# Attention scores on halves of the TensorE array, with PSUM banks split 4/2/2

## The chip, the cores and the metric

The kernel runs on one core of a Trainium2 chip. The core has five engines that work side by side and meet through semaphores: TensorE (PE, matrix products into PSUM), VectorE (DVE), ScalarE (ACT), GpSimd (POOL) and SyncE (SP, which issues DMAs). PSUM has eight banks of 2 KB per partition; every matmul result lands in one of them and must be read out by DVE or ACT before the bank can be used again. The metric is the device time of one execution in microseconds; three runs of the kernel before gave 281.81, 282.52 and 284.34 us, median 282.52.

## The reference

Two layers follow each other. The first is attention with 4 batches, 8 heads, 768 positions and head size 64, in which a query sees the 8 first keys (global) and the 96 latest ones (local), with a bias by distance:

```python
scores = scale * np.matmul(q, k.transpose(0, 1, 3, 2))
keep = is_global | is_local          # key < 8, or 0 <= query - key < 96
bias = -slopes[:, None, None] * dist[None, :, :]
scores = np.where(keep, scores + bias, -1e9)
a = softmax(scores)                  # over the keys
x = np.matmul(a, v)                  # then heads side by side: 768 x 512 per batch
```

The second mixes positions by a matrix of rank 32 and then channels by a feed-forward of width 2048:

```python
h = x.transpose(0, 2, 1) @ U @ V
u = x + h.transpose(0, 2, 1)
out = u + np.maximum(u @ w_ch1, 0.0) @ w_ch2
```

## The kernel before, in words

The work unit of the attention is a pair of heads of one batch, 16 pairs in all, four per batch. Keys run along partitions. A pair's q and k arrive as 128 positions by (head, 64) tiles; `st_T` transposes six blocks of q and six of k on PE (line 223) into two PSUM tiles `tp`, so that head 0 lies on partitions 0 to 63 and head 1 on 64 to 127. DVE copies the k tile whole into `kT` (L230) and builds `kA` from it (L231, L232), which holds for each off-diagonal block the local keys with the eight global ones put in front. The q tile is copied into two zero-padded tiles: ACT copies head 0 into the upper half of `qz..0` (L229), DVE copies head 1 into the lower half of `qz..1` (L235); the other halves were set to zero once. So a score matmul for one head can contract over all 128 partitions of `kT`, both heads' keys, and the zeros drop the other head.

A head has 11 score blocks of 128x128: six diagonal (L263, from `kT`) and five beside the diagonal (L268, from `kA`), written into `sc` tiles of up to four blocks, so three chunks per head. For pairs 4 to 15 (batches 1 to 3) `st_S` evicts each chunk on DVE with scale and bias into `sp` (L294), `st_E` takes the exp of a head on ACT (L302, into `ep`), and `st_V` multiplies `ep` with the values (L314, L318, into `ob`), divides by the sum and writes x (L323, L325, L328). For pairs 0 to 3 (batch 0) `st_SE` adds the bias with a matmul over all 128 rows and takes the exp straight from PSUM.

`st_M1` and `st_M2` do the low-rank mix (`tmp_ps` L336, `ups` L347 and L352; the results `uT` go out on DVE for one half of the positions, L358, and on ACT for the other, L360). The feed-forward of a batch is a queue of units: 32 up units of four `hps` matmuls (L376) and a relu on ACT (L380, into `htr`), and 24 down units of `cps` matmuls (L389, L395), four units to a token tile, which ends with an addition on DVE (L401) and a store.

PSUM tiles come from three pools: `sc` (scores) with three banks, `oc` (`ob`, `cps`) with two, `th` (`tp`, `tmp_ps`, `ups`, `hps`) with three. A pool's banks go round in the order of allocation; an operation that needs a bank waits until its last reader is done.

Batch 0 is issued in the order in which it is written. After `ordered.close()` a scheduler orders the instructions of each engine ahead of time; the program loops over pairs 4 to 15, and `fill` puts feed-forward units of the batch before between the steps of the attention. What runs on the chip is then a fixed order per engine; PE executes its matmuls in that order. After the last pair the feed-forward of batch 3 runs alone: per half batch 16 up units in a row, then 12 down units.

Of the kernel before, what the change touches and what calls it, by code (L numbers as in the profile page):

```python
# [11 lines left out]
FP32 = mybir.dt.float32  # L12
FP16 = mybir.dt.float16
# [3 lines left out]
ALU = mybir.AluOpType  # L17
# [3 lines left out]
def kernel(  # L21
# [13 lines left out]
    nc = tc.nc  # L35
    B, H, S, D = q.shape
    NG = int(n_global)
    NL = int(n_local)
    P = 128
    DM = H * D  # L40
    NSB = S // P
# [4 lines left out]
    NP = H // 2  # L46
    qk_scale = 1.0 / math.sqrt(D)
# [5 lines left out]
    slope = [2.0 ** (-8.0 * (h + 1) / H) for h in range(H)]  # L53
# [5 lines left out]
    W = 256 * NSB - P  # L59
# [6 lines left out]
    kp = ctx.enter_context(tc.tile_pool(name="kp", bufs=2))  # L66
    scp = ctx.enter_context(tc.tile_pool(name="scp", bufs=2))
# [3 lines left out]
    psum = ctx.enter_context(tc.tile_pool(name="psum", bufs=1, space=bass.MemoryType.PSUM))  # L71

    def ps_sc():
        return psum.tile([P, 512], FP32, name="sc", tag="sc", bufs=3)

    def ps_oc(name):
        return psum.tile([P, 512], FP32, name=name, tag="oc", bufs=2)

    def ps_th(name, dtype=FP32, cols=512):
        return psum.tile([P, cols], dtype, name=name, tag="th", bufs=3)  # L80


    NVB = 4
# [30 lines left out]

    NPAIR = B * NP
    staged, cast, vts = {}, {}, {}


    ordered = ExitStack()
# [9 lines left out]
    def warm(n):  # L129
# [12 lines left out]
        out=relB, in_=relB, compare_op=ALU.is_ge, fill=BIG,  # L142
# [3 lines left out]
        out=relB, in_=relB, compare_op=ALU.is_ge, fill=BIG,  # L146
# [24 lines left out]
    relcat = cst.tile([P, 3, 256], FP32, name="relcat")  # L171
# [39 lines left out]
    kts, kas, vas = {}, {}, {}  # L211

    def st_T(i):
        stq, stk = cast.pop(i)
        kT = kp.tile([P, S], FP16, name="kT", tag="kT")
        kA = kp.tile([P, NSB - 1, P], FP16, name="kA", tag="kA")
        tps = []
        for st in (stq, stk):

            tp = ps_th("tp", FP16, S)  # L220
            tps.append(tp.rearrange("d (n p) -> d p n", n=NSB))
            for n in range(NSB):
                nc.tensor.matmul(  # L223
                    tp[:, n * P:(n + 1) * P], st[:, n].rearrange("s h d -> s (h d)"), ident16,
                    is_transpose=True, start=(n == 0), stop=(n == NSB - 1),
                )
        tq, tk = tps
        z = qz[i % 2]
        nc.scalar.copy(z[0][0:D].rearrange("d (p n) -> d p n", n=NSB), tq[0:D])  # L229
        nc.vector.tensor_copy(kT.rearrange("d (p n) -> d p n", n=NSB), tk)  # L230
        nc.vector.tensor_copy(kA.rearrange("d n p -> d (n p)"), kT[:, 0:S - P])  # L231
        nc.vector.tensor_copy(  # L232
            kA[:, 1:, 0:NG], kT[:, 0:NG].unsqueeze(1).broadcast_to((P, NSB - 2, NG))
        )
        nc.vector.tensor_copy(z[1][D:P].rearrange("d (p n) -> d p n", n=NSB), tq[D:P])  # L235
        kts[i], kas[i] = kT, kA
# [11 lines left out]
    sps, eps = {}, {}  # L248

    def scores(i, hi, c, on_pe):  # L250
        h = 2 * (i % NP) + hi
        kT, kA, z = kts[i], kas[i], qz[i % 2][hi]
        sc = ps_sc()
        c0 = 512 * c
        tot = min(512, W - c0)
        r0 = 256 if c else 0
        if on_pe:
            nc.tensor.matmul(
                sc[:, 0:tot], slI[:, h], rel16.rearrange("p a c -> p (a c)")[:, r0:r0 + tot], start=True, stop=False
            )  # L260
        for kb in (2 * c, 2 * c + 1):
            o = 256 * kb - c0
            nc.tensor.matmul(  # L263
                sc[:, o:o + P], kT[:, kb * P:(kb + 1) * P], z[:, kb * P:(kb + 1) * P],
                start=(o == 0 and not on_pe), stop=(o + P == tot),
            )
            if kb < NSB - 1:
                nc.tensor.matmul(  # L268
                    sc[:, o + P:o + 2 * P], kA[:, kb], z[:, (kb + 1) * P:(kb + 2) * P],
                    start=False, stop=(o + 2 * P == tot),  # L270
                )
        return sc, c0, tot, r0
# [10 lines left out]
            )  # L283

    def st_S(i, c):
        if c == 0:
            sps[i] = [
                scp.tile([P, W], FP32, name=f"sp{hi}", tag=f"sp{hi}", bufs=1)
                for hi in range(2)
            ]  # L290
        relf = relcat.rearrange("p a c -> p (a c)")
        for hi in range(2):
            sc, c0, tot, r0 = scores(i, hi, c, False)
            nc.vector.scalar_tensor_tensor(  # L294
                out=sps[i][hi][:, c0:c0 + tot], in0=sc[:, 0:tot],
                scalar=qk_scale / slope[2 * (i % NP) + hi], in1=relf[:, r0:r0 + tot],
                op0=ALU.mult, op1=ALU.add,
            )
# [32 lines left out]
    def st_M1(i):  # L331
        b, dc = i // NP, i % NP
        ch = slice(dc * P, (dc + 1) * P)
        tps = ps_th("tmp_ps")
        for n in range(NSB):
            nc.tensor.matmul(  # L336
                tps[:, 0:P], u16[:, n], x16s[b][:, n, ch],
                start=(n == 0), stop=(n == NSB - 1),
            )
        nc.vector.tensor_copy(tmps[b][:, ch], tps[:, 0:P])  # L340

    def st_M2(i):
        b, dc = i // NP, i % NP
        ch = slice(dc * P, (dc + 1) * P)
        for g in range(2):
            ups = ps_th("ups")
            nc.tensor.matmul(  # L347
                ups[:, 0:GT], tmps[b][:, ch], v16w[:, g * GT:(g + 1) * GT],
                start=True, stop=False,
            )  # L350
            for t in range(NTG):
                nc.tensor.matmul(  # L352
                    ups[:, t * P:(t + 1) * P], x16s[b][:, NTG * g + t, ch], ident16,
                    start=False, stop=(t == NTG - 1),
                )
            dst = uTs[b][:, dc, g * GT:(g + 1) * GT]
            if g == 0:
                nc.vector.tensor_copy(dst, ups[:, 0:GT])  # L358
            else:
                nc.scalar.copy(dst, ups[:, 0:GT])  # L360
# [56 lines left out]
    new_batch(0)  # L417
    cast_qk(0, nc.vector)
    st_T(0)
    warm(2)  # L420
    cast_qk(1, nc.vector)
# [6 lines left out]
    for i in range(NP):  # L428
# [12 lines left out]
        if i:  # L441
            cast_qk(i + 2, nc.gpsimd)
        st_SE(i, 1)
        st_T(i + 1)
        if i < 3:
            slopes(2 * i + 2, 2 * i + 4)
# [27 lines left out]
    for i in range(NP, NPAIR):  # L474
# [6 lines left out]
        for c in range(3):  # L481
            st_S(i, c)
            fill(1)
# [8 lines left out]
        if i + 1 < NPAIR:  # L492
            if hp == NP - 1:
                new_batch(b + 1)
            st_T(i + 1)
# [48 lines left out]
```

## Time and profile before

| what | value |
|---|---|
| three runs, us | 281.81, 282.52, 284.34 |
| span of the profiled execution, us | 279.8 |
| PE busy, us | 255.3 (91%) |
| DVE busy, us | 147.8 (53%) |
| ACT busy, us | 123.2 (44%) |
| POOL busy, us | 87.2 (31%) |
| mean granted PE clock | 0.963 |

The span runs from the first to the last instruction of the profiled execution; its own device time is not listed, the median of the three runs is 2.7 us above the span. The page gives, for each group of instructions, the line, the engine, the operation, what it writes and reads, the count, then busy time in us, the mean duration in ns, and the idle time of the engine just before with what ended it. Matmuls are pipelined: the 228 ns of a score matmul is from its start to its modelled end, while the next one may start 56 ns later. In the timeline each row has its start and duration in us. About 57 us pass until batch 0 is through; from there to 232.8 us attention and feed-forward share PE, and the last 47 us are feed-forward alone.

### The profile page before, as it was taken

The page shows a single profiled execution, that of the slowest core. Times are in us where ns is not written, and L with a number is a line of the kernel's source. Part 1 is how long each engine was busy: PE and PEld are TensorE (multiplying, and loading weights), DVE is VectorE, ACT ScalarE, POOL GpSimd, SP SyncE. Part 2 cuts the span into 40 slices and gives each one's busy share as a digit, 9 for nine tenths or more (in the row PEclk, how much of TensorE's full clock was granted, in tenths as well). Part 3 has the DMA queues.
Part 4 walks back from the last instruction along what each step waited for, and adds up shares of the span by engine and source line. Part 5 has one row for each costly group of instructions (what it writes and reads, how often), then busy time and mean ns, then how long its engine had stood idle before and what let it go on. Part 6 is the DMA issues. An engine that isn't in the chain of part 4 may idle for free.

```text
span 279.8 us, 5080 instructions
## 1 busy us (share of the span) xinstructions
PE 255.3 (91%) x2076; PEld 156.1 (56%) x2076; DVE 147.8 (53%) x301; ACT 123.2 (44%) x209; POOL 87.2 (31%) x129
## 2 busy tenths in 40 slices
PE   7765775899998999799999999999999999999994
PEld 3544554566556655566456655675566555545541
DVE  6766799156666564755957575754574440010011
ACT  2434551565218650668037630856076604604700
POOL 8948688360425124330606042300200010000000
PEclk9779896699999999999999999999999999999999
DMA  6999999992462527170634023000110021001001
GB/s 220 277 281 181 198 233 235 227 239 25 150 105 15 128 63 152 55 127 2 164 79 40 2 43 64 37 2 0 75 41 0 2 76 40 0 37 75 2 37 75
DMA packets 42327, 26.64 MB, mean 95 GB/s; under 512 B 26912, under 2 KB 39232, under 8 KB 42304
## 3 DMA queue, kind: packets, MB, share of 16 engines
q0 software_dynamic: 30144, 7.44, 27.5%
q1 hardware_dynamic: 12160, 18.88, 20.0%
q8 instruction: 16, 0.26, 0.4%
q14 instruction: 7, 0.06, 0.1%
HBM read 27.46 MB, written 6.29 MB: 121 GB/s over the span
## 4 chain that ended last, share of the span: by engine, by line
PE 62%; DVE 8%; ACT 4%; issue 2%; ACTq 0%
PE hps L376 25%; PE cps L395 24%; ACT ep L302 3%; PE tp L223 3%; DVE sp L294 2%; PE sc L268 2%; PE cps L389 2%; PE sc L263 2%; DVE qz L235 2%; DVE kT L230 2%; DVE osb L401 1%; PE tmp_ps L336 1%; PE ob L318 1%; PE ups L352 1%; PE ups L347 1%
## 5 line engine op out<-in xcount | busy, mean ns | idle before, releaser
L376 PE MATMUL hps<-uT,w 128*128 128x384 f16 x512 | 93.4, 328 | 1.3 <-DVE uT L358 1.3
L395 PE MATMUL cps<-w,htr 128*128 128x512 f16 x384 | 91.3, 379 | 0.0
L380 ACT ACTIVATE htr<-hps 128x384 f16<-128x384 f32 x128 | 61.8, 491 | 55.8 <-PE hps L376 55.1
L376 PEld LDWEIGHTS <-w 128*128 128x128 f16 x512 | 48.9, 98 | 30.7 <-issue 3.8
L395 PEld LDWEIGHTS <-htr 128*128 128x128 f16 x384 | 36.1, 98 | 37.4 <-issue 0.4
L302 ACT ACTIVATE ep<-sp 128x1408 f16<-128x1408 f32 x24 | 31.7, 1368 | 39.5 <-DVE sp L294 39.5
L294 DVE SCALAR_TENSOR_TENSOR sp<-sc,relcat 128x512 f32<-128x512 f32 (+1 forms) x72 | 41.8, 637 | 8.6 <-PE sc L268 8.3
L401 DVE TENSOR_TENSOR osb<-cps,x_sb 128x512 f32<-128x512 f32 x24 | 16.6, 690 | 49.6 <-PE cps L395 49.4
L110 POOL DMA_DIRECT2D v<-in_v_dram x32 | 27.3, 857 | 26.1 <-PE ob L318 13.9
L328 POOL CAST x<-x_sb 128x384 f16<-128x384 f32 x32 | 16.4, 514 | 52.5 <-DVE x_sb L325 52.3
L263 PE MATMUL sc<-qz,kT 128*128 128x128 f16 x192 | 30.4, 228 | 1.7 <-DVE qz L235 1.3
L230 DVE COPY kT<-tp 128x768 f16<-128x768 f16 x16 | 15.3, 957 | 28.0 <-PE tp L223 28.0
L268 PE MATMUL sc<-qz,kA 128*128 128x128 f16 x160 | 27.6, 230 | 1.9 <-DVE kA L231 1.3
L102 POOL CAST q<-qst 128x768 f16<-128x768 f32 x14 | 11.6, 830 | 56.8 <-issue 51.5
L268 PEld LDWEIGHTS <-kA 128*128 128x128 f16 x160 | 16.5, 103 | 10.5 <-issue 2.8
L318 PE MATMUL ob<-v,ep 128*128 128x65 f16 x192 | 17.9, 200 | 4.6 <-ACT ep L302 4.4
L263 PEld LDWEIGHTS <-kT 128*128 128x128 f16 x192 | 19.2, 103 | 4.6 <-DVE qz L235 0.9
L318 PEld LDWEIGHTS <-ep 128*128 128x128 f16 x192 | 14.6, 102 | 9.0 <-ACT ep L302 5.4
L281 ACT ACTIVATE ep<-sc 128x512 f16<-128x512 f32 (+1 forms) x24 | 12.6, 562 | 15.3 <-PE sc L268 15.1
L360 ACT CAST uT<-ups 128x384 f16<-128x384 f32 x16 | 7.5, 469 | 26.8 <-PE ups L352 26.8
L325 DVE TENSOR_TENSOR x_sb<-ob,rcp 128x384 f32<-128x384 f32 x32 | 17.7, 553 | 0.6
L314 PE MATMUL ob<-vA,ep 128*128 128x65 f16 x160 | 15.5, 200 | 0.9 <-POOL vA L241 0.5
(60 smaller groups left out, 236.9 us busy)
## 6 DMA issues: line engine op xcount, KB each, us to landing
qst<-in_q_dram SPq DMA_DIRECT2D x16, 384.0 KB, 5.7
kst<-in_k_dram SPq DMA_DIRECT2D x16, 384.0 KB, 6.1
out_dram<-osb SPq DMA_DIRECT2D x24, 256.0 KB, 2.0
w<-in_moe_w_ch_dram POOLq DMA_DIRECT2D x8, 512.0 KB, 11.9
v<-in_v_dram POOLq DMA_DIRECT2D x32, 96.0 KB, 6.2
u<-in_moe_U_dram POOLq DMA_DIRECT2D x1, 48.0 KB, 12.8
v16w<-in_moe_V_dram POOLq DMA_DIRECT2D x1, 48.0 KB, 11.4
```

The lines of the kernel that those rows point to most:

```text
L110: nc.gpsimd.dma_start(vt[:, hi, :, 0:D], v[b, h0 + hi].rearrange("(n p) d -> p n d", p=P))
L230: nc.vector.tensor_copy(kT.rearrange("d (p n) -> d p n", n=NSB), tk)
L263: nc.tensor.matmul(sc[:, o:o + P], kT[:, kb * P:(kb + 1) * P], z[:, kb * P:(kb + 1) * P], start=(o == 0 and not on_pe), stop=(o + P == tot),)
L268: nc.tensor.matmul(sc[:, o + P:o + 2 * P], kA[:, kb], z[:, (kb + 1) * P:(kb + 2) * P], start=False, stop=(o + 2 * P == tot),)
L294: nc.vector.scalar_tensor_tensor(out=sps[i][hi][:, c0:c0 + tot], in0=sc[:, 0:tot], scalar=qk_scale / slope[2 * (i % NP) + hi], in1=relf[:, ...
L302: nc.scalar.activation(ep, sps[i][hi], AF.Exp, scale=slope[2 * (i % NP) + hi])
L318: nc.tensor.matmul(ob[:, qi], ep[:, DG[qi]:DG[qi] + P], vt[:, hi, qi], start=(qi == 0), stop=True,)
L325: nc.vector.tensor_tensor(xo, ob[:, :, 0:D], rcp.unsqueeze(2).broadcast_to((P, NSB, D)), ALU.mult)
L376: nc.tensor.matmul(hps[:, 0:GT], w1_16[:, dc, jt * P:(jt + 1) * P], uT[:, dc, ts], start=(dc == 0), stop=(dc == NDC - 1),)
L380: nc.scalar.activation(cell["htr"][:, jt], hps[:, 0:GT], AF.Relu)
L395: nc.tensor.matmul(cps, htr[:, jc, t * P:(t + 1) * P], w2_16[:, jc], start=False, stop=(jc == NJC - 1),)
L401: nc.vector.tensor_tensor(osb, cps, x_sb[:, n], ALU.add)
```

## The change

In pairs 4 to 15 the padded query tiles are gone. `st_T` copies the q tile once, all 128 partitions, on ACT into a new tile `qT` (two buffers); DVE copies `kT` as before; a new function `st_G` builds `kA` with the same two copies. `st_S2` takes the place of `st_S`: it allocates both heads' `sc` tiles of a chunk together and issues the blocks with the two heads alternating. Each matmul contracts over 64 partitions, head 0 on rows 0 to 63 of the array and head 1 on rows 64 to 127; all other matmuls still span 128 rows. Batch 0 keeps the padded tiles. Pool `sc` gets four banks in place of three, `th` two in place of three.

```diff
     def ps_sc():
-        return psum.tile([P, 512], FP32, name="sc", tag="sc", bufs=3)
+        return psum.tile([P, 512], FP32, name="sc", tag="sc", bufs=4)
     def ps_th(name, dtype=FP32, cols=512):
-        return psum.tile([P, cols], dtype, name=name, tag="th", bufs=3)
+        return psum.tile([P, cols], dtype, name=name, tag="th", bufs=2)
+    headT = {}
+
+    def st_G(i):
+        qT, kT = headT[i]
+        kA = kp.tile([P, NSB - 1, P], FP16, name="kA", tag="kA")
+        nc.vector.tensor_copy(kA.rearrange("d n p -> d (n p)"), kT[:, 0:S - P])
+        nc.vector.tensor_copy(
+            kA[:, 1:, 0:NG], kT[:, 0:NG].unsqueeze(1).broadcast_to((P, NSB - 2, NG))
+        )
+        kas[i] = kA
...
         tq, tk = tps
+        if i >= NP:
+            qT = kp.tile([P, S], FP16, name="qT", tag="qT")
+            nc.scalar.copy(qT.rearrange("d (p n) -> d p n", n=NSB), tq)
+            nc.vector.tensor_copy(kT.rearrange("d (p n) -> d p n", n=NSB), tk)
+            headT[i] = qT, kT
+            st_G(i)
+            return
...
     def st_S(i, c):
+        if i in headT:
+            return st_S2(i, c)
...
+    def st_S2(i, c):
...
+        scs = [ps_sc(), ps_sc()]
+        half = [slice(0, D), slice(D, P)]
+        for kb in (2 * c, 2 * c + 1):
+            o = 256 * kb - c0
+            for hi in range(2):
+                nc.tensor.matmul(
+                    scs[hi][:, o:o + P], kT[half[hi], kb * P:(kb + 1) * P],
+                    qT[half[hi], kb * P:(kb + 1) * P],
+                    start=(o == 0), stop=(o + P == tot),
+                )
+            if kb < NSB - 1:
+                for hi in range(2):
+                    nc.tensor.matmul(
+                        scs[hi][:, o + P:o + 2 * P], kA[half[hi], kb],
+                        qT[half[hi], (kb + 1) * P:(kb + 2) * P],
+                        start=False, stop=(o + 2 * P == tot),
+                    )
+        for hi in range(2):
+            nc.vector.scalar_tensor_tensor(
+                out=sps[i][hi][:, c0:c0 + tot], in0=scs[hi][:, 0:tot],
+                scalar=qk_scale / slope[2 * (i % NP) + hi], in1=relf[:, r0:r0 + tot],
+                op0=ALU.mult, op1=ALU.add,
+            )
```

More of the change, by code (lines that the diff above doesn't have):

```diff
@@ L215, in st_T @@
         kT = kp.tile([P, S], FP16, name="kT", tag="kT")
-        kA = kp.tile([P, NSB - 1, P], FP16, name="kA", tag="kA")
         tps = []
@@ L227, in st_T @@
         tq, tk = tps
+        if i >= NP:
[5 more added lines that the diff above has]
+            return
+        kA = kp.tile([P, NSB - 1, P], FP16, name="kA", tag="kA")
         z = qz[i % 2]
@@ L295, in st_S @@
                 out=sps[i][hi][:, c0:c0 + tot], in0=sc[:, 0:tot],
+                scalar=qk_scale / slope[2 * (i % NP) + hi], in1=relf[:, r0:r0 + tot],
+                op0=ALU.mult, op1=ALU.add,
+            )
+    def st_S2(i, c):
+        if c == 0:
+            sps[i] = [
+                scp.tile([P, W], FP32, name=f"sp{hi}", tag=f"sp{hi}", bufs=1)
+                for hi in range(2)
+            ]
+        relf = relcat.rearrange("p a c -> p (a c)")
+        qT, kT = headT[i]
+        kA = kas[i]
+        c0 = 512 * c
+        tot = min(512, W - c0)
+        r0 = 256 if c else 0
+        scs = [ps_sc(), ps_sc()]
[18 more added lines that the diff above has]
+                out=sps[i][hi][:, c0:c0 + tot], in0=scs[hi][:, 0:tot],
                 scalar=qk_scale / slope[2 * (i % NP) + hi], in1=relf[:, r0:r0 + tot],
```

## The prediction

> **What bounds the kernel now.** I read the page's busy shares first, then the table of 40 slices, then the costliest groups, then the busy times of chosen stretches, and last the timeline, for distances between starts.
>
> ```profile
> span 279.8 us, 5080 instructions
> ...
> PE 255.3 (91%) x2076; PEld 156.1 (56%) x2076; DVE 147.8 (53%) x301; ACT 123.2 (44%) x209; POOL 87.2 (31%) x129
> ...
> PE   7765775899998999799999999999999999999994
> ...
> L263 PE MATMUL sc<-qz,kT 128*128 128x128 f16 x192 | 30.4, 228 | 1.7 <-DVE qz L235 1.3
> ...
> L268 PE MATMUL sc<-qz,kA 128*128 128x128 f16 x160 | 27.6, 230 | 1.9 <-DVE kA L231 1.3
> ```
>
> From the ninth slice (57 us) on TensorE (PE) is the bound; before it, in batch 0, it is not. The times in the group rows (228 ns for a score matmul) overlap and can't be added. What a matmul takes from the stream is the distance to the next start:
>
> ```profile
> 155.35 0.22 PE L263 MATMUL sc<-qz,kT 128*128 128x128 f16 x1
> 155.41 0.22 PE L268 MATMUL sc<-qz,kA 128*128 128x128 f16 x1
> 155.46 0.81 PE L376 MATMUL hps<-uT,w 128*128 128x384 f16 x4
> ...
> 116.18 0.19 PE L318 MATMUL ob<-v,ep 128*128 128x65 f16 x1
> 116.21 0.20 PE L314 MATMUL ob<-vA,ep 128*128 128x65 f16 x1
> 116.24 0.19 PE L318 MATMUL ob<-v,ep 128*128 128x65 f16 x1
> ```
>
> A score matmul takes 56 ns, an `ob` matmul with a new 128x128 weight each time 30 ns; by the same reading 162 ns for `hps`, 216 for `cps`, 163 for the wide `ups`, 56 for every other 128-column one.
>
> Batches 1 to 3 repeat a turn of two head pairs, with half a batch of feed-forward beside it; six turns:
>
> ```profile
> 145.32:175.29 29.97, 29.66 (x258) 18.33 (x256) 19.24 (x38) 14.66 (x25) 9.81 (x14) 1.00 0.28 41
> ```
>
> Columns: stretch, length, busy PE, weight loads, DVE, ACT, POOL, granted clock, DMA share, GB/s. The clock is full. The stream of a turn: 64 `hps` 10.37, 51 `cps` 11.02, 44 scores 2.46, 44 `ob` 1.32, 48 other 128-column matmuls 2.69, 4 wide `ups` 0.65: 28.51 us. So PE waits 1.46 us in a turn, and what the change saves or adds there goes to the end nearly one to one.
>
> **The score matmuls.** 264 of the 352 change (12 pairs x 22). Two neighbours now use different halves of the array and different banks. No row shows two matmuls side by side. Bounds from rows: 30 ns each, the `ob` distance, which holds a full weight load; and 103 ns each, the weight-load row of these lines, if each load stood in the open; 56 is no change. I take 30: a stream that issues load and matmul at that rate is in this trace. 44 x 26 ns = 1.14 us saved in a turn, 6.9 us in six.
>
> **The boundaries.** In the changed order the scores stand in 44 stretches of 1 to 22 matmuls between full-array work, 8 in a turn, so 16 boundaries a turn. Every matmul before spans 128 rows, so no row shows a boundary. Lower bound 0. Upper bound: the array must run empty: 219 ns from start to modelled end less the 56 to the next start, 163 ns. Restarting an empty PE costs little here (after a wait the first `ob` matmuls start 39 ns apart instead of 29). I take the middle, 82 ns: the modelled end holds the write to PSUM, which need not be waited for. 16 x 82 = 1.31 us a turn, of which about 0.4 falls into waits that stand there anyway: 0.9.
> The Trainium skill speaks for the upper bound: "TensorEngine Tiling (Array Packing)", Key Properties, says that a change of tiling mode, as against a change of tile, drains TensorE. The same list says that tiles work independently. No run here shows either yet. With a full drain the boundaries would cost 2.6 us a turn by the bound above, more than the overlap can give.
>
> **Two banks where three were.** `th` serves transposes, `tmp_ps`, `ups` and `hps`.
>
> ```profile
> 156.31 0.49 ACT L380 ACTIVATE htr<-hps 128x384 f16<-128x384 f32 x1 [0.61 <-PE hps L376]
> ...
> 114.92 0.55 DVE L358 CAST uT<-ups 128x384 f16<-128x384 f32 x1
> 115.52 0.48 PE L376 MATMUL hps<-uT,w 128*128 128x384 f16 x2 [1.34 <-DVE uT L358]
> ```
>
> The `hps` group that starts at 155.46 is read by ACT from 156.31 to 156.80: its bank is held 1.34 us. A release reaches PE 0.05 us after the reader's end (115.47 to 115.52). With two banks the next but one group starts 1.40 us later; four `hps` matmuls take 0.65, two groups 1.30. So an unbroken run of `hps` loses 0.10 us every second group. The last two runs have 16 groups each: 7 x 0.10 x 2 = +1.4 us after 232.8 us, where nothing covers it.
> Inside a turn I followed the changed order by hand with these durations. Waits of PE, us:
> - `ob` right behind `ups`. The exp that it needs starts 1.9 us after the second chunk's scores (172.55 to 174.46) and takes 1.36; PE has two times four `cps`, six scores and `ups` (2.5 us) in between: 0.8. Before, eight `hps` stood there. The second head's exp: 0.3.
> - The run of eight `hps`: 0.3, the first two behind the transposes' evictions 0.1, the one behind `tmp_ps` 0.3.
> - `ups` second half 0.2, the `hps` behind it 0.1 (its bank waits for DVE's `uT`, queued behind six 0.57 us `sp` operations); transposes of k 0.2 and 0.3 (both banks are taken by `hps`, whose relus stand behind two exps on ACT); small ones 0.1.
> - Scores of the next pair, for kT and kA: 0.5, much as now (164.84 and 165.19: 0.54).
>
> Sum 3.1 against 1.46 now: +1.6 us a turn. `sc` has a fourth bank, but with six evictions of 0.57 us per 22 scores DVE sets that pace: nothing.
>
> **The removed copy.** 12 of DVE's 64x768 copies go (961 ns each, 11.5 us of DVE). ACT's copy widens from 64 to 128 partitions at no cost: DVE's 128-partition kT copy takes 957 ns, its 64-partition twin 961. The copy sat behind kT and ahead of kA on DVE, and late kA is a wait of PE at 134.4, 164.8 and 194.8; that gain is in the list above, kA comes about 1 us earlier. What is late next there is kT itself. Also at pair 4 the chain qz, scores, `sp`, exp is some 0.5 us shorter; in batch 0 `ups` must wait once for the still padded copy (+0.2): -0.3 together. POOL and SP keep their instructions; loads and stores change places by a few, at a DMA share of 0.07 to 0.42 in the turns. The pool of the new query tile costs no time.
>
> **The sum**, against this execution: a turn -1.14 + 1.6 + 0.9 = +1.4; six turns +8.4; the end +1.4; batch 0 -0.3: **+9.5 us**, span 289.3. The three runs' median, 282.52, is 2.7 above the profiled span; on it that is **292.0 us**, 3.4% slower. A measurement of this kernel tells about 1% from no change.
>
> **The rivals.**
> - *Overlap wins* (the other side): the halves run side by side with free boundaries and the two banks cost PE no more waiting than now. Place: the eight stretches of a turn. 27.37 + 1.46 = 28.83 us a turn, -6.9 + 1.4 - 0.3 = -5.8: **276.7**. It decides when boundaries and added waits together stay under 0.96 us a turn. For it: PE is the bound and waits little. Against: the bank arithmetic, two 0.65 groups against 1.40.
> - *Free boundaries, waits as listed*: +0.5 a turn, +4.1: **286.6**.
> - *Full drain* at 163 ns: 2.6 a turn less 0.6 hidden: +2.5, six turns +15, +16.1: **298.6**.
> - *It doesn't do what it says*: the two halves follow each other at 56 ns. Nothing saved: +1.6 a turn without a boundary cost (10.7, **293**), and with a full drain +3.6 (22.7, **305**). With loads in the open (103 ns) and free boundaries 44 x 47 ns + 1.6 less 0.2 hidden is +3.5 a turn (**304**). For it: each matmul still brings its own 128-column weight load.
>
> **How the numbers follow.** Forecast 0.36, overlap wins 0.18, free boundaries 0.15, full drain 0.20, no overlap 0.11. The hand-followed waits are good to some 0.4 us a turn, 2.5 us in all, which spreads each case. Faster by over 1% (under 279.7): most of the overlap case, 0.15. Within 1%: its rest and the lower part of free boundaries, 0.11. Slower: 0.74. The range 279 to 303 leaves out most of the overlap case and the ends at 304 and 305, together under 0.2.
>
> **What would show it.** Steps: alternating score starts 30 ns apart or less on average (not 56); at each boundary a start distance 80 ns longer than the form's own, on both sides; in the last 47 us `hps` groups 0.70 apart on average, every second one waiting for ACT's relu; waits of `ob` for exp of about 0.8 us, once in a turn; DVE busy near 136 us; a turn of 31.4 us in place of 29.97. I am wrong if boundaries show no gap, if the `hps` runs keep 0.65, or if the scores keep 56 ns.

## The result, and the profile after

The changed kernel takes 295.48 us (median; 294.59 to 298.52) against 282.59 us for the kernel before, timed beside it: a ratio of 1.048 with an interval of 1.041 to 1.054. It is slower by 4.8%; the forecast was 292.0 us and the range 279 to 303. The profiled execution spans 292.9 us, 13.1 more than before; the forecast had put 9.5 more.

The page of the changed kernel, its busy shares, PE's row of the 40 slices and the groups of the feed-forward's first product and its relu (columns as above):

```profile
span 292.9 us, 5087 instructions
...
PE 260.1 (89%) x2074; PEld 145.3 (50%) x2076; DVE 138.6 (47%) x289; ACT 124.3 (42%) x209; POOL 87.3 (30%) x129
...
PE   7575673999988999799998999899999999999994
...
L431 PE MATMUL hps<-uT,w 128*128 128x384 f16 x512 | 96.9, 328 | 4.4 <-DVE kT L240 2.8
...
L435 ACT ACTIVATE htr<-hps 128x384 f16<-128x384 f32 x128 | 62.7, 490 | 69.6 <-PE hps L431 69.4
```

The first of these groups in the kernel before:

```profile
L376 PE MATMUL hps<-uT,w 128*128 128x384 f16 x512 | 93.4, 328 | 1.3 <-DVE uT L358 1.3
```

DVE lost 9.2 us of work (147.8 to 138.6) and PE, the bound, gained idle time: its share fell from 91% to 89% of a longer span, and the `hps` group that used to wait 1.3 us now waits 4.4, most of it for DVE's copy `kT`.

The busy times of two turns, and of the stretch from the last wide `ups` to the end (columns: stretch, length, then busy PE, weight loads, DVE, ACT, POOL, granted clock, DMA share, GB/s):

```profile
150.64:183.29 32.65, 30.73 (x258) 16.52 (x256) 17.27 (x36) 14.95 (x25) 9.99 (x14) 1.00 0.26 37
183.29:215.23 31.94, 30.73 (x259) 16.51 (x256) 16.62 (x36) 14.95 (x25) 5.09 (x8) 1.00 0.07 26
...
241.57:292.90 51.33, 47.26 (x249) 23.67 (x246) 5.40 (x8) 16.16 (x33) 0.00 (x0) 0.99 0.11 42
```

The number of matmuls in a turn is what it was (258), DVE has two copies fewer, and the turn is 2.0 to 2.7 us longer than the 29.97 us of before. The turns are counted from one wide `ups` to another: from 51.53 us in the kernel before and 51.68 in the changed one to the last wide `ups`, at 229.90 and 241.57. The 13.1 us are in three places:

| place | before, us | after, us | difference | forecast |
|---|---|---|---|---|
| start to the first turn | 51.53 | 51.68 | +0.15 | -0.3 |
| six turns | 178.37 | 189.89 | +11.5 | +8.4 |
| the end | 49.90 | 51.33 | +1.4 | +1.4 |

Now the starts. The timeline of PE around one stretch of eight score matmuls in the changed kernel (columns: start and duration in us, engine, line, operation, how many in a row):

```profile
163.71 0.82 PE L431 MATMUL hps<-uT,w 128*128 128x384 f16 x4
164.47 0.23 PE L336 MATMUL sc<-qT,kT 64*128 64x128 f16 x2
164.53 0.22 PE L343 MATMUL sc<-qT,kA 64*128 64x128 f16 x2
164.59 0.22 PE L336 MATMUL sc<-qT,kT 64*128 64x128 f16 x2
164.65 0.22 PE L343 MATMUL sc<-qT,kA 64*128 64x128 f16 x2
164.80 0.82 PE L431 MATMUL hps<-uT,w 128*128 128x384 f16 x4
```

"x2" is a pair, one matmul per head. The pairs start 60 ns apart: two matmuls take the time that one took (in the records of the turn at 183.29 the two of a pair start 3 ns apart and the next pair 53 or 54 ns later, so 57 ns per pair). And the two edges cost something: the last of the four `hps` starts at 164.21, so the first score follows after 258 ns where an `hps` takes 162, and the next `hps` follows the last scores after 148 ns where 56 would do. Beside it, the weight loads (PEld) of the same place:

```profile
163.89 0.26 PEld L431 LDWEIGHTS <-w 128*128 128x128 f16 x2
164.46 0.10 PEld L336 LDWEIGHTS <-kT 64*128 64x128 f16 x2 [0.32 <-issue]
164.48 0.10 PEld L343 LDWEIGHTS <-kA 64*128 64x128 f16 x2
```

The loads of the last two `hps` start while the matmul ahead of them runs. The load of the first score starts only 4 ns before its own matmul, after 0.32 us in which nothing was loaded.

### The profile page after: what moved, and what is told of

Same layout as the page of the kernel before. It is cut to its first block, busy times and chain, and to the rows that moved or that the text cites. A ratio compares the mean times of both kernels' runs of the same rounds, so it can differ in the third digit from the quotient of the medians.

```text
span 292.9 us, 5087 instructions
## 1 busy us (share of the span) xinstructions
PE 260.1 (89%) x2074; PEld 145.3 (50%) x2076; DVE 138.6 (47%) x289; ACT 124.3 (42%) x209; POOL 87.3 (30%) x129
## 4 chain that ended last, share of the span: by engine, by line
PE 62%; DVE 15%; issue 11%; POOL 5%; ACT 4%; DMA 1%; SPq 0%; ACTq 0%; POOLq 0%; DVEq 0%
PE hps L431 27%; PE cps L450 21%; DVE sp L349 5%; ACT ep L357 3%; PE tp L232 2%; DVE kT L240 2%; PE cps L444 2%; POOL vA L258 2%; PE ob L373 2%; DVE x_sb L380 1%; PE tmp_ps L391 1%; DMA kst<-in_k_dram 1%; PE ob L369 1%; POOL v L110 1%; DVE vA L259 1%
## 5 line engine op out<-in xcount | busy, mean ns | idle before, releaser
L431 PE MATMUL hps<-uT,w 128*128 128x384 f16 x512 | 96.9, 328 | 4.4 <-DVE kT L240 2.8
L450 PE MATMUL cps<-w,htr 128*128 128x512 f16 x384 | 93.8, 380 | 0.0
L431 PEld LDWEIGHTS <-w 128*128 128x128 f16 x512 | 47.9, 97 | 42.4 <-issue 11.9
L102 POOL CAST q<-qst 128x768 f16<-128x768 f32 x14 | 11.9, 853 | 48.7 <-issue 47.4
L373 PE MATMUL ob<-v,ep 128*128 128x65 f16 x192 | 19.3, 204 | 5.4 <-ACT ep L357 5.0
L240 DVE COPY kT<-tp 128x768 f16<-128x768 f16 x12 | 11.4, 953 | 19.0 <-PE tp L232 19.0
L395 DVE CAST tmp<-tmp_ps 128x128 f16<-128x128 f32 x16 | 4.6, 288 | 32.7 <-PE tmp_ps L391 32.7
L369 PE MATMUL ob<-vA,ep 128*128 128x65 f16 x160 | 16.6, 204 | 0.8 <-POOL vA L258 0.7
L378 DVE RECIPROCAL rcp<-ob 128x6 f32<-128x6 f32 x32 | 6.1, 190 | 20.5 <-PE ob L373 20.4
L275 PE MATMUL sc<-rel,slI 128*128 128x512 bf16 (+1 forms) x22 | 9.4, 426 | 7.0 <-DVE slI L172 7.0
L258 POOL COPY vA<-v 128x650 f16<-128x650 f16 x16 | 11.8, 737 | 12.4 <-issue 8.6
## 6 DMA issues: line engine op xcount, KB each, us to landing
w<-in_moe_w_ch_dram POOLq DMA_DIRECT2D x8, 512.0 KB, 11.9
```

What stands on the lines that cost most here:

```text
L258: nc.gpsimd.tensor_copy(vA, vt[:, :, 0:NSB - 1])
L369: nc.tensor.matmul(ob[:, qi], ep[:, OF[qi - 1]:OF[qi - 1] + P], vA[:, hi, qi - 1], start=True, stop=False,)
L373: nc.tensor.matmul(ob[:, qi], ep[:, DG[qi]:DG[qi] + P], vt[:, hi, qi], start=(qi == 0), stop=True,)
L431: nc.tensor.matmul(hps[:, 0:GT], w1_16[:, dc, jt * P:(jt + 1) * P], uT[:, dc, ts], start=(dc == 0), stop=(dc == NDC - 1),)
L450: nc.tensor.matmul(cps, htr[:, jc, t * P:(t + 1) * P], w2_16[:, jc], start=False, stop=(jc == NJC - 1),)
```

## The experiments

**The halves without the banks.** The changed kernel with the split of the kernel before:

```diff
-        return psum.tile([P, 512], FP32, name="sc", tag="sc", bufs=4)
+        return psum.tile([P, 512], FP32, name="sc", tag="sc", bufs=3)
-        return psum.tile([P, cols], dtype, name=name, tag="th", bufs=2)
+        return psum.tile([P, cols], dtype, name=name, tag="th", bufs=3)
```

> The halves alone, with the old banks 3/2/3; the scheduler's order has 47 stretches of scores (94 boundaries), 17 of them three matmuls of one head. Theory (overlap is real, a boundary costs 95 ns, two `th` banks are the larger part of the loss): overlap -5.9 us, boundaries +8.9, kA waits -0.5, no bank waits and 0.65 us per `hps` group at the end: 285 us. Rival, the loss is all in the boundaries: near 294. Rival, the banks hide a gain of the halves: 277.

Measured: 283.54 us against 281.37 beside it, ratio 1.006 (1.002 to 1.010). Busy times of a turn in this run:

```profile
176.91:207.01 30.10, 30.10 (x258) 16.78 (x256) 17.56 (x36) 14.71 (x25) 5.25 (x8) 1.00 0.07 27
```

30.10 us is within 0.13 of the kernel before. So the halves by themselves neither win nor lose much: over the six turns this run takes 180.59 us against 178.37, 2.2 us more. The larger part of the 4.8% needs the bank split (`sc` and `th` are both set back here). The end is 49.87 us in this run, as before (49.90): the +1.4 us there belong to the banks.

**The banks without the halves.** The kernel before with four `sc` and two `th` banks:

```diff
-        return psum.tile([P, 512], FP32, name="sc", tag="sc", bufs=3)
+        return psum.tile([P, 512], FP32, name="sc", tag="sc", bufs=4)
-        return psum.tile([P, cols], dtype, name=name, tag="th", bufs=3)
+        return psum.tile([P, cols], dtype, name=name, tag="th", bufs=2)
```

> The banks alone: padded scores over 128 rows with banks 4/2/2, no boundary anywhere. Theory: the banks by themselves cost 10 to 14 us, 293 to 297, with `hps` groups 0.70 us apart at the end. Rival, boundaries are the loss: 283 to 285, only the end of the feed-forward slower by 1.4 us.

Measured: 300.54 us, ratio 1.067 (1.061 to 1.072); 3.5 us above the upper end of what was expected, and slower than the changed kernel, which has the same banks. A turn takes 33.34 us.

**Which of the two pools.** The same with `sc` left at three, one bank unused:

```diff
-        return psum.tile([P, cols], dtype, name=name, tag="th", bufs=3)
+        return psum.tile([P, cols], dtype, name=name, tag="th", bufs=2)
```

> The kernel before with two `th` banks and nothing else changed (one bank idle). Theory (`th` alone carries the cost of the bank split): within 1.5% of the 300.5 us of the padded kernel with 4/2/2. Rival, the fourth `sc` bank's effect on the scheduler's order carries it: 282 to 287, with only the end slower.

Measured: 300.98 us, ratio 1.064 (1.060 to 1.069), the same as with four `sc` banks. With padded queries the third `th` bank carries the whole price, and the fourth `sc` bank gives nothing back; with the halves the two pools were not changed apart. Why it is dearer with padded queries is told by PE's waits of this run between 57 and 235 us (what waited and for what: us in total, times, longest):

```profile
PE hps L376 <- DVE kT L230: 6.3, 5, 2.7
PE ob L318 <- ACT ep L302: 2.6, 5, 0.8
PE sc L263 <- DVE qz L235: 2.3, 3, 0.8
```

and by DVE's timeline in it (a bracket gives the idle time before, and what ended it):

```profile
156.51 0.61 DVE L242 COPY vA<-v 8x520 f16<-8x520 f16 x1 [1.32 <-POOL vA L241]
157.05 0.17 DVE L323 RECIPROCAL rcp<-ob 128x6 f32<-128x6 f32 x1
157.26 0.56 DVE L325 TENSOR_TENSOR x_sb<-ob,rcp 128x384 f32<-128x384 f32 x1
157.73 0.94 DVE L230 COPY kT<-tp 128x768 f16<-128x768 f16 x1
158.71 0.96 DVE L235 COPY qz<-tp 64x768 f16<-64x768 f16 x1
```

With two banks the transposes of q and k fill the whole pool, and the next `hps` has no bank until one of them is copied out. Here both copies, kT and the padded qz, stand one behind the other on DVE, 1.9 us in all; in the changed kernel q is ACT's alone, and its bank comes free without DVE. So these waits speak for the single q copy, against a loss that the two banks bring; no run moves that copy alone.

**The wait for kT in the changed kernel.** Its own waits of PE between 57 and 235 us, with the same columns:

```profile
PE hps L431 <- DVE kT L240: 2.8, 4, 0.9
PE ob L373 <- ACT ep L357: 2.2, 4, 0.8
PE hps L431 <- DVE uT L413: 1.5, 1, 1.5
```

One case of the first line, in the timeline of PE:

```profile
157.14 1.14 PE L431 MATMUL hps<-uT,w 128*128 128x384 f16 x6 [0.92 <-DVE kT L240]
```

what DVE did just before, in its timeline:

```profile
154.92 0.61 DVE L259 COPY vA<-v 8x520 f16<-8x520 f16 x1 [1.31 <-POOL vA L258]
155.46 0.17 DVE L378 RECIPROCAL rcp<-ob 128x6 f32<-128x6 f32 x1
155.67 0.56 DVE L380 TENSOR_TENSOR x_sb<-ob,rcp 128x384 f32<-128x384 f32 x1
156.14 0.95 DVE L240 COPY kT<-tp 128x768 f16<-128x768 f16 x1
```

and what POOL did, which DVE waited for:

```profile
153.33 0.83 POOL L110 DMA_DIRECT2D v<-in_v_dram  x1 [8.43 <-PE ob L373]
154.15 0.74 POOL L258 COPY vA<-v 128x650 f16<-128x650 f16 x1
```

From the bottom up: POOL issues the load of a later v only when PE's `ob` has freed the buffer, then copies the values for the next pair (`vA`, L258); DVE's small copy into the same tile (L259) waits 1.31 us for that; kT stands behind it on DVE; and PE waits 0.92 us for kT's bank. To take this wait away, the small copy goes to POOL, where it stands behind L258 in any case:

```diff
-        nc.vector.tensor_copy(
+        nc.gpsimd.tensor_copy(
             vA[0:NG, :, 1:],
```

> The changed kernel with the small copy of the global values (8 x 520) on POOL in place of DVE, so that DVE's queue no longer waits there for POOL ahead of kT. Theory: the waits of `hps` for kT (2.8 us in four) go: 292.5 us. Rival, kT is late for its own sake or the wait moves to another reader: 295 to 296.

Measured: 293.68 us, ratio to the kernel before 1.043 (1.034 to 1.051), where the changed kernel has 1.048 (1.041 to 1.054). PE's waits of this run between 57 and 235 us:

```profile
PE ob L373 <- ACT ep L357: 2.7, 5, 0.8
PE hps L431 <- DVE uT L413: 1.5, 1, 1.5
```

and the busy times of one of its turns:

```profile
182.87:214.56 31.69, 30.69 (x258) 16.50 (x256) 16.29 (x34) 14.95 (x25) 6.13 (x10) 1.00 0.07 26
```

The line for kT is gone, so the chain through POOL was its cause. In the profiled executions the six turns take 187.87 us instead of 189.89, so 2.0 us come of the 2.8 that the line held. In the whole time this isn't settled: batch 0 took 1.3 us longer in that execution (53.02 us against 51.68), the span is only 1.1 us shorter, and the two intervals overlap. The other waits stay, and the turn shown is still 1.7 us over 29.97.

**Without the alternation.** The changed kernel with all blocks of head 0 of a chunk ahead of those of head 1:

```diff
-        for kb in (2 * c, 2 * c + 1):
+        for kb, hi in [(kb, hi) for hi in range(2) for kb in (2 * c, 2 * c + 1)]:
...
-            for hi in range(2):
+            if True:
```

> The changed kernel with a chunk's blocks in the order head 0, then head 1, so that neighbours are mostly on the same half; the same 44 stretches, and nearly the same order of everything else. Theory (neighbours on different halves run side by side, 3 and 53 ns, on the same half 56 ns): most of 7 us is lost, 300 to 302 us. Rival, score matmuls are hidden behind the waits anyway: within 1% of the changed kernel, 295.

Measured: 295.28 us, ratio 1.047 (1.042 to 1.053): no difference, where the theory had expected 300 to 302. The timeline of PE around one stretch of eight shows why:

```profile
165.48 0.24 PE L336 MATMUL sc<-qT,kT 64*128 64x128 f16 x2
165.54 0.23 PE L343 MATMUL sc<-qT,kA 64*128 64x128 f16 x2
165.60 0.23 PE L336 MATMUL sc<-qT,kT 64*128 64x128 f16 x2
165.66 0.23 PE L343 MATMUL sc<-qT,kA 64*128 64x128 f16 x2
165.82 0.82 PE L431 MATMUL hps<-uT,w 128*128 128x384 f16 x4
```

The program now says L336, L343, L336, L343 for head 0 and then the same for head 1. The record has L336 twice, then L343 twice: the two of a pair start 13 or 14 ns apart, and from the last `hps` before to the first behind pass 0.60 us, where the alternating order takes 0.59. So here the edit did not take the overlap away: the second head's matmuls started beside the first's though they stand four places behind. It did so only in short stretches, where three matmuls are all of head 0 and start 67 and 56 ns apart; of the 264 scores, 107 pairs start together, against 119 in the changed kernel.

A scheduler stands between the program and PE, and the record doesn't list the order that it handed over. Two things speak for head 0 having stood first: those stretches of three hold head 0's L336, L343, L336 alone, and the lag inside a pair grows with the matmuls that stand between, 3 ns where the heads alternate, 10 in the stretches of six, 13 or 14 in those of eight. The run therefore can't say whether the overlap is worth anything; the next three do.

**Overlap and boundary, each alone.** The kernel before, with four matmuls of 128 columns added behind each of the last 32 `hps` groups. The results of these 128 matmuls are used by nothing. They contract over 128 rows, over the same 64 rows, or over the two halves in turn:

```diff
+                if b == B - 1:
+                    if jt == 0:
+                        cell["dm"] = [ps_sc(), ps_sc()]
+                    for n, r in enumerate(ROWS):
+                        nc.tensor.matmul(cell["dm"][n % 2][:, 0:P],
+                            w1_16[r, 0, 0:P], uT[r, 0, 0:P], start=True, stop=True)
```

with ROWS = four times `slice(0, P)`; four times `slice(0, D)`; `slice(0, D), slice(D, P)` twice.

> The kernel before, with four matmuls more behind each of the last 32 `hps` groups: 128 rows, 128 columns, into two idle score banks, their results not used. This is the measure for the next two, which have the same order of instructions. 128 x 56 ns: the last feed-forward is 7.2 us longer.

> The same 128 added matmuls, each over the first 64 rows: 33 stretches, 66 boundaries, no overlap possible; results not used. Theory (a boundary costs 95 ns each way, neighbours on one half take 56 ns): 6.3 us longer than with 128 rows. Rival, what the changed kernel shows at the boundaries is a wait for its operands: no longer than with 128 rows.

> The same 128 added matmuls over 64 rows, taking the two halves in turn, each half with its own bank; results not used. Theory (two halves side by side): 64 x 53 ns = 3.4 us shorter than with one half, so 2.9 us longer than with 128 rows. Rival, the halves' starts stand together in the record but the work does not overlap: as long as with one half.

Each ran once: 289.94, 295.30 and 295.75 us. Batch 0 came out up to 4 us apart in these single executions, so they are compared from the last wide `ups` to the end, where only `hps`, `cps` and the added matmuls run. Busy times of that stretch in the kernel before, with nothing added:

```profile
229.90:279.80 49.90, 45.90 (x249) 23.83 (x246) 5.40 (x8) 16.16 (x33) 0.00 (x0) 1.00 0.11 43
```

with full rows:

```profile
231.24:288.20 56.96, 52.93 (x375) 30.90 (x372) 5.40 (x8) 16.19 (x33) 0.00 (x0) 1.00 0.10 38
```

with one half:

```profile
229.85:293.50 63.65, 59.65 (x375) 28.24 (x372) 5.39 (x8) 16.16 (x33) 0.00 (x0) 1.00 0.09 34
```

and with the two halves in turn:

```profile
233.76:293.90 60.14, 56.20 (x375) 24.84 (x372) 5.40 (x8) 16.19 (x33) 0.00 (x0) 1.00 0.10 36
```

Of the added matmuls 126 fall into this stretch. Full rows cost 7.06 us, 56 ns each. One half costs 6.69 us more; nothing differs but the rows, so 64 boundaries (32 stretches, two each) cost **105 ns apiece**. The matmuls themselves aren't dearer on one half: inside a stretch they follow each other after 66, 56 and 56 ns, while the first comes 258 ns after the `hps` ahead of it. Two halves in turn cost 3.51 us less than one half: 63 pairs save 56 ns each, so a pair takes the time of one matmul. Both figures agree with the starts in the changed kernel. There the boundary shows as 96 ns at the entry (258 less 162) and 92 at the exit (148 less 56), with about 10 ns more on the second start on either side. What the 105 ns consist of isn't shown. An array that runs empty is one reading; a weight load that can't run ahead across the edge is another, since a load takes 93 to 99 ns in this record and the first one of a stretch starts beside its matmul instead of ahead of it. No run separates the two.

**Longer stretches.** With these prices a stretch of eight alternating matmuls saves 8 x 28 = 224 ns and pays two boundaries, 210 ns. Stretches longer than that should then win. Two units of feed-forward behind each chunk and none behind the exps, with three `sc` and three `th` banks, leave 41 stretches instead of 47, so 6.4 scores in a stretch on average instead of 5.6: nearer to eight, but not beyond it. The same moves in the kernel before show what they are worth without the halves:

```diff
             st_S(i, c)
-            fill(1)
+            fill(2)
...
-        fill(2)
+        fill(0)
...
         st_M1(i)
-        fill(1)
+        fill(0)
```

> The halves with banks 3/2/3, and two feed-forward units behind each chunk of scores in place of one (none behind the exps), which leaves the scheduler 41 stretches of scores in place of 47 and nearly all of them alternating. Theory (105 ns per boundary all told, 28 ns per matmul that finds a partner): 12 boundaries less, -1.3 us, and the lost partners back, -1.4 us: 280.5 to 282, within 1% of the kernel before. Rival, the boundaries can be had for less in longer stretches: clearly faster than before, under 279.

> The kernel before with the same two units behind each chunk: what the moved units do by themselves. Theory: PE is the bound and its stream is the same, so within 1% of the kernel before. Rival, the units now missing behind the exps uncover them, 0.5 us a pair: 286 to 288.

Measured: 280.37 us with halves, ratio 0.994 (0.991 to 0.997), and 280.43 us with padded queries, ratio 0.995 (0.993 to 0.998). Both beat the kernel before by half a per cent, and each other not at all. The gain is the moved units', not the halves'. Whether stretches of well over eight would win was not run.

## Why the prediction came out as it did

The direction was right, and its main reason too: the third `th` bank is worth more than the halves can give. The turn at 183.29, with its own time of 31.94 us, can be set against the forecast turn, step by step:

| step of the prediction | forecast, us a turn | measured |
|---|---|---|
| overlap, 44 scores | -1.14 (30 ns each) | -1.17 (21 pairs, 56 ns saved by each; 2 found no partner) |
| boundaries, 16 | +1.31, of which 0.4 hidden: +0.9 | 1.68 (105 ns each), of which 0.3 hidden: +1.4 |
| waits | 3.1 against 1.46: +1.6 | 3.2 against 1.5: +1.8 |
| turn | +1.4 | +2.0 |

**The step that was mis-sized is the boundary.** The prediction put 82 ns, the middle of its bounds; it costs 105. That part of it falls into waits was right: 3 of the 16 boundaries of this turn do. One of them, in the timelines of ACT and of PE:

```profile
194.09 0.49 ACT L435 ACTIVATE htr<-hps 128x384 f16<-128x384 f32 x1 [0.25 <-PE hps L431]
194.41 0.22 PE L343 MATMUL sc<-qT,kA 64*128 64x128 f16 x1
194.63 0.81 PE L431 MATMUL hps<-uT,w 128*128 128x384 f16 x4
```

The relu ends at 194.58 and the `hps` that needs its bank starts 0.05 us later, the time that a release takes without a boundary too. So what shows is 1.4 us a turn where 0.9 were put, 0.5 of the 0.6 by which this turn was missed. "TensorEngine Tiling (Array Packing)" of the Trainium skill, Key Properties, which says that a change of tiling mode drains TensorE, pointed the right way: there is a cost at every edge. The size is the trace's: 105 ns, under the 163 ns of the prediction's bound for an array run empty, so the full-drain rival's price was too dear. The time alone could not have told: 295.48 us lies between the forecast, 292.0, and that rival, 298.6, and slightly nearer to the rival.

**The list of waits** held in sum, and term by term but for three. (As written its terms add up to 3.2, not 3.1.) `ob` behind `ups` waited 0.65 us in this turn (0.8 forecast), the second exp 0.27 (0.3), the run of eight `hps` 0.28 (0.3), the transposes of k 0.16 and 0.25 (0.2 and 0.3), the second half of `ups` 0.20 (0.2). The `hps` behind `tmp_ps` took 0.17 instead of 0.3, and the scores for kT and kA 0.75 instead of 0.5; the hidden boundaries lie in these two. "Behind the transposes' evictions 0.1" was wrong: it was 0.38 us here and about 1 us in the two turns before. The hand-followed order left out that kT stands behind the small vA copy and, through it, behind POOL.

**Six equal turns** were too simple. Over the six the changes were +1.0, +1.9, +2.6, +2.7, +2.0 and +1.4 us. The third and fourth, dearer than the fifth by 0.6 and 0.7, are those in which the wait for kT was 1.02 and 1.09 us instead of 0.38. The sixth has 22 scores in four stretches, half of what the prediction put there; 22 of the 264 lie ahead of the first turn. In all, the six turns have 86 boundaries, 16 of them hidden, and 111 pairs. By the measured prices, which is an estimate, 70 boundaries cost 7.4 us where 5.4 were put, and 111 pairs save 6.2 us where 6.8 were put. These two make up 2.6 of the 3.1 us by which the turns were missed.

**The end** was right to the tenth: +1.4 us, and for the reason given. Relus of the changed kernel in the last part (timeline of ACT):

```profile
251.60 0.49 ACT L435 ACTIVATE htr<-hps 128x384 f16<-128x384 f32 x1 [0.16 <-PE hps L431]
252.34 0.49 ACT L435 ACTIVATE htr<-hps 128x384 f16<-128x384 f32 x1 [0.24 <-PE hps L431]
252.99 0.49 ACT L435 ACTIVATE htr<-hps 128x384 f16<-128x384 f32 x1 [0.16 <-PE hps L431]
253.73 0.49 ACT L435 ACTIVATE htr<-hps 128x384 f16<-128x384 f32 x1 [0.24 <-PE hps L431]
```

They start 0.74, 0.65 and 0.74 us apart: two groups in 1.39 us, where the prediction had worked out 1.40 from the time that a bank is held, and where 1.30 is what the matmuls alone need.

**The removed copy** gave DVE 9.2 us. What it gave PE isn't shown by itself: with three banks the changed kernel is 0.6% slower than the one before. An estimate from the prices: the six turns of that run have 90 boundaries, 84 of them not hidden in a wait (8.8 us), and 83 pairs (4.6 us saved), which would make them 4.2 us longer; they are 2.2 us longer. So some 2 us came back from elsewhere, perhaps from the earlier kA. Two `th` banks cost 6.4% with padded queries. Between the changed kernel and its version with three banks lie 295.48 - 283.54 = 11.9 us, 4.2%. Whether batch 0 gained the 0.3 us of the forecast can't be told, since it differs by up to 4 us between executions.

**The rivals.** *Overlap wins* fell: its condition was that boundaries and added waits stay under 0.96 us a turn, and boundaries alone show 1.4; even with the third bank kept, the halves don't win. *Free boundaries* fell by the 105 ns, *no overlap* by the 3.51 us that the two halves saved over one. Of *full drain* the price of 163 ns fell; whether the array runs empty at an edge is open.

What stays open: what the 105 ns of a boundary consist of, how much of the whole time the wait for kT costs (its removal is clear in the list of waits and in the six turns, but not in the times), what the removed copy is worth alone, and why the first turn lost less than the others.

## What to carry to other kernels

Matmuls on the two halves of the array do run side by side, but each edge to full-array work costs 105 ns here, so they call for few, long stretches: at 28 ns saved per matmul of 128 columns, eight in a stretch only break even. That longer ones win follows from these two prices; no run here had them. Before a bank is moved from one pool to another, add up how long a bank of that pool is held (matmuls, the reader's wait and its run) and divide by the banks: two banks held 1.40 us can't follow groups of 0.65. When a pool shrinks to what one step fills at once (here q and k transposes), whatever stands ahead of that step's evictions on their engine, and behind whom, becomes a wait of TensorE.

## What the runs showed of the hardware that was not expected

- The order in the program didn't bind the two halves to each other. With four matmuls of head 0 ahead of four of head 1 the starts came in pairs 13 or 14 ns apart (10 with three ahead of three), and the time was that of the alternating order (295.28 and 295.48 us). "TensorE: Matmul & The Clock Gate" of the Trainium skill, Part 3, says that matmuls start strictly in program order; the record of this run differs, if the scheduler handed PE the order of the program, for which the two signs above speak. The start lag that the same part gives for tiles beside each other, about 4 ns, is near the 3 ns between the two matmuls of an alternating pair.
- A boundary costs the same whether the array goes from 128 rows to 64 or back (96 and 92 ns at the first start), and both edges leave some 10 ns on the start after that.
- Two halves with a new weight load of 64x128 each take 57 ns a pair, the price of one full-array matmul of 128 columns (56 ns): the weight loads of the two halves did not add to it.
